# Weight loads of the late blocks, whole and in four pieces

## The chip, the cores and the metric

The kernel runs on one core of a Trainium2 chip, as one launch. The metric is the device time of that launch in microseconds (us); three runs of the kernel before gave 556.94, 559.24 and 561.79 us, median 559.24. The core has five engines that run side by side and meet at semaphores: TensorE (PE, with its weight loads as PEld), VectorE (DVE), ScalarE (ACT), GpSimd (POOL) and SyncE (SP, which here only issues transfers). Transfers run on 16 DMA engines, from two queues that matter here: q1, filled by SP, and q0, filled by POOL.

## The reference

An attention without a score matrix feeds a mixture of experts of which each token uses one. There are 8 batches of 576 tokens, 8 heads of 64, so 4608 tokens of 512 numbers, and 8 experts.

```python
kv = np.einsum('bhsd,bhse->bhde', k_s, v)          # k_s: softmax of k over the tokens
x  = np.einsum('bhsd,bhde->bhse', q_s, kv)         # q_s: softmax of q over its 64 numbers
for b in range(B):                                 # x as (B, S, 512)
    prev_e = -1
    for s in range(S):
        fresh_e = argmax(logits[b, s])             # logits = x @ w_gate
        e = fresh_e if s == 0 or local_gate[b, s] < 0.5 else (prev_e if prev_e >= 0 else fresh_e)
        prev_e = e
        h = np.maximum(x[b, s] @ w1[e], 0.0)       # w1[e]: 512 x 1024, 2 MB in f32
        out[b, s] = p[e] * (h @ w2[e])             # w2[e]: 1024 x 512, 2 MB; p: softmax of logits
```

## The kernel before

Tokens are sorted by expert into blocks of 128 rows, each of one expert. The first NA = 9 blocks hold tokens of the first half and run between pieces of the attention, in an order written out in the table ORDER; the other blocks (b = 9 and up) run one after the other in `block(b)`, from b = 36 on inside nested `If`s that ask whether the block exists. The profile shows some 30 of these late blocks.

A product in f32 is made of f16 pieces: a weight w becomes w1h + w1l (or w2h + w2l), an activation a high and a low part. One block on PE is `ffn1(b,0)`, the second half of the block before (`ffn2(b-1,1)`), `ffn1(b,1)`, `ffn2(b,0)`. `ffn1` stands in an `If` on PE (line 889): a block whose expert has at most 64 rows left in it takes a body with 64 columns, all others the body behind it with 128. So PE jumps once per half. ACT and DVE make the hidden layer's pair (`act_hi`, line 911; `act_lo`, line 915) and POOL gathers rows for block b + 4 (`gather`, 844), the gates (`gather_share`, 850) and scatters the result (`put`, 933). SP turns the rows of block b + 3 by a transposing transfer (`turn_dma`, line 880, tile xT), which needs `prep_lo` (DVE, line 867).

The f32 weights of the next expert wait in two staging tiles of 2 MB, s1 for w1 and s2 for w2. Where a block starts a new expert, `renew(b, pieces)` turns the 16 pieces of 256 KB (128 columns of s1 each, 0 to 7; a 128-row chunk in s2 each, 8 to 15) into the f16 pairs, on ACT (line 190) and DVE (line 955), in an `If` on the flag of the block; otherwise it is jumped over. The pieces 0 to 9 of block b + 1 are renewed during block b (`next_`), 10 to 15 during block b + 1 itself. `fetch(b, i)` is the load of staging tile i with the expert that comes after that of block b; it is issued by SP in every block with a condition (block b starts an expert and another follows), and moves nothing where the condition is 0. In `block(b)` both fetches stand at the end, as 2 MB each: s2 of block b, then s1 of block b + 1. The transfer of s1 for block 9 (`fetch(9, 1)`) is issued from the table ORDER.

SP, like every engine, takes its instructions in order: a transfer whose wait isn't over holds all transfers behind it. On SP each DMA row of the program waits for the engines named behind it (`DVE`, `Activation`) and for earlier transfers (`DMAHW0` to `DMAHW7`, counters that SP's transfers use in turn).

Of the kernel before, what the change touches and what calls it, by code (L numbers as in the profile page):

```python
# [15 lines left out]
ET = mybir.EngineType  # L16
# [4 lines left out]
NE = 8  # L21
# [9 lines left out]
NBM = NBF + NE - 1  # L31
NA = 9
NB = NBM - NA
NP = NA
# [121 lines left out]
def moe_kernel(ctx, tc, q, k, v, w_gate, w_local, w1, w2, out, dbg=None):  # L156
    nc = tc.nc
# [11 lines left out]
    W, plan = {}, []  # L169
# [10 lines left out]
    def at(pair, b):  # L180

        return pair[0][:, b] if b < NA else pair[1][:, b - NA]
# [614 lines left out]

    outr = out.rearrange("b s d -> (b s) d")
    xg, xn, x2, xT, pb, pt, py, hi, lo, ys, ph = ([] for _ in range(11))
    fst, e0, few, phs = {}, {}, {}, {}  # L800
    AHEAD, NPB = 4, 4

    def turns(pool, to, n, shape, dt, name):
# [33 lines left out]
    def word(w_, hi_, engines):  # L837
        return nc.values_load(w_, min_val=0, max_val=hi_, engines=engines,
                              skip_runtime_bounds_check_because="clamped where it is worked out")

    def gather(b):
        src = xrows[0:2 * 1152, :] if b < NA else xrows
        i_, j_ = (gidx[0], b) if b < NA else (gidx[1], b - NA)
        nc.gpsimd.indirect_dma_start(out=xg[b % AHEAD], out_offset=None, in_=src,  # L844
                                     in_offset=bass.IndirectOffsetOnAxis(ap=i_[:, j_:j_ + 1], axis=0))

    def gather_share(b):
        src = shares[0:2 * 1152, :] if b < NA else shares
        i_, j_ = (gidx[0], b) if b < NA else (gidx[1], b - NA)
        nc.gpsimd.indirect_dma_start(out=pb[b % NPB], out_offset=None, in_=src,  # L850
                                     in_offset=bass.IndirectOffsetOnAxis(ap=i_[:, j_:j_ + 1], axis=0))
# [7 lines left out]
    def prep_hi(b):  # L859
        copy(on("Ph", b) if ("Ph", b) in plan[0].tasks else nc.scalar, x2[b % 2][:, 0, :], xn[b % 2], XS)  # L860

    def prep_lo(b):
        if ("Pl", b) in plan[0].tasks and on("Pl", b) is nc.gpsimd:
            nc.gpsimd.tensor_scalar(out=xn[b % 2], in0=xn[b % 2], scalar1=XS, scalar2=None, op0=ALU.mult)
            nc.gpsimd.tensor_tensor(out=x2[b % 2][:, 1, :], in0=xn[b % 2], in1=x2[b % 2][:, 0, :], op=ALU.subtract)
        else:
            nc.vector.scalar_tensor_tensor(out=x2[b % 2][:, 1, :], in0=xn[b % 2], scalar=XS, in1=x2[b % 2][:, 0, :],  # L867
                                           op0=ALU.mult, op1=ALU.subtract)
# [10 lines left out]
    def turn_dma(b):  # L879
        nc.sync.dma_start(out=xT[b % 4].rearrange("p i c t -> p (i c) t"), in_=x2[b % 2].rearrange("p i d -> p (i d)"),  # L880
                          transpose=True)

    def ffn1(b, g):
        if b < NA:
            hidden(b, g, P)
            return
        if g == 0:
            few[0] = word(at(info, b)[:, 5:6], 1, [ET.PE])
        with tc.If(few[0] == 1) as cmp:
            hidden(b, g, P // 2)  # L890
        with cmp.Else():
            hidden(b, g, P)
# [25 lines left out]
    def result(b):  # L918

        return py[0 if b < NP else (b - NP + 1) % 2]  # L920

    def ffn2(b, g):
        hi_, lo_ = hi[b % 2], lo[b % 2]
        for f in range(4 * g, 4 * g + 4):
            for i, (h_, w_) in enumerate(((hi_, W["w2h"]), (hi_, W["w2l"]), (lo_, W["w2h"]))):
                nc.tensor.matmul(result(b), h_[:, f, :], w_[:, f, :], start=(f == 0 and i == 0), stop=(f == 7 and i == 2))  # L926

    def give(b):
        nc.scalar.activation(ys[b % 2], result(b), AF.Copy, scale=pb[b % NPB])

    def put(b):
        i_, j_ = (sidx[0], b) if b < NA else (sidx[1], b - NA)
        nc.gpsimd.indirect_dma_start(out=outr, out_offset=bass.IndirectOffsetOnAxis(ap=i_[:, j_:j_ + 1], axis=0),  # L933
                                     in_=ys[b % 2], in_offset=None, bounds_check=NT - 1, oob_is_err=False)
# [8 lines left out]
    def cut_hi(i, eng=None):  # L943
        s_, h_, _ = piece(i)
        copy(eng or on("Wh", i), h_, s_, WS)

    def cut_lo(i, eng=None):
        s_, h_, l_ = piece(i)
        if (eng or on("Wl", i)) is nc.gpsimd:
            sh = list(s_.shape)  # L950
            nc.gpsimd.tensor_tensor(out=s_, in0=s_, in1=wsc.unsqueeze(2).to_broadcast(sh) if i < 8 else wsc.to_broadcast(sh),
                                    op=ALU.mult)
            nc.gpsimd.tensor_tensor(out=l_, in0=s_, in1=h_, op=ALU.subtract)
        else:
            nc.vector.scalar_tensor_tensor(out=l_, in0=s_, scalar=WS, in1=h_, op0=ALU.mult, op1=ALU.subtract)
# [11 lines left out]
    def flag(b):  # L967
        fst[b] = word(at(info, b)[:, 0:1], 1, [ET.Activation, ET.DVE])

    def renew(b, pieces):  # L970
        with tc.If(fst[b] == 1):  # L971
            for i in pieces:
                cut_hi(i, nc.scalar)
                cut_lo(i, nc.vector)
# [3 lines left out]
            flag(b)  # L978
        renew(b, range(4 * k, 4 * k + 4))

    def fetch(b, i):

        if b >= NBM - 1:
            return
        s_, src = ((W["s1"], w1_src), (W["s2"], w2_src))[i - 1]
        w_ = at(info, b)
        cond, e = w_[:, 4:5], w_[:, 1:2]
        if NX0 <= b < NA:
            cond, e = w_[:, 2:3] if b == NX0 else w_[:, 0:1], w_[:, 3:4]
        kw = dict(cond=(word(cond, 1, [ET.SP]) == 1), cond_hint=False)  # L990
        nc.sync.dma_start(out=s_, in_=src(bass.ds(word(e, NE - 1, [ET.SP]), 1)), **kw)

    pl = Plan(dict(kt=NKT, vt=NVT, km=2, mt=2, kb=2, vp=2, pk=1, psq=2, px=1, pz=2, qt=NQT, qs=3, qe=NQE, xt=NXT, kvT=2, rs=3, cs=1,
                   qm=3, ex=2, xg=AHEAD, xn=2, x2=2, xT=4, pst=1, psh=2, psy=1, hh=2, y=2, dl=1, pb=NPB),
# [92 lines left out]
    for b in range(NP + 4):  # L1087
# [17 lines left out]
        if b > 0:  # L1105
            for i in range(2 if b == NP else 4):
                src = [("F1", b - 1, 0), ("F1", b - 1, 1), ("F2", b - 1, 0), ("F2", b - 1, 1)][i]
                add(("RN", b, i), ACT, renew4, after=[src, ("aj",) if b < NA else ("bj",)], order=[("s1" if i < 2 else "s2", b - 1)])
            add(("s1", b), SP, lambda b: fetch(b, 1), after=[("RN", b, 0), ("RN", b, 1)] + ([("bj",)] if b >= NX0 else []))
        else:  # L1110
            add(("s1", b), SP, lambda b: fetch(b, 1), after=[("Wl", i) for i in range(8)] + [("aj",)], order=[("W", 3)])
        if b == NP:
            continue
        add(("s2", b), SP, lambda b: fetch(b, 2),
            after=([("RN", b, 2), ("RN", b, 3)] if b else [("Wl", i) for i in range(8, 16)] + [("aj",)]) + ([("bj",)] if b >= NX0 else []))
        for g in range(2):
# [15 lines left out]
    def prep_a(b):  # L1132
        if b < NBM:
            prep_x(b)

    def prep_b(b):
        if b < NBM:
            prep_hi(b)
            prep_lo(b)

    def act(b, g):
        act_hi(b, g)
        act_lo(b, g)

    def next_(b, pieces):
        if b + 1 < NBM:
            renew(b + 1, pieces)

    def block(b):


        if b + AHEAD < NBM:
            gather(b + AHEAD)
        prep_a(b + 3)
        if b + 1 < NBM:
            gather_share(b + 1)
            if b + 1 not in fst:
                flag(b + 1)
        ffn1(b, 0)
        act(b, 0)  # L1160
        renew(b, FROM[b][0])
        next_(b, (0, 1))
        ffn2(b - 1, 1)
        ffn1(b, 1)
        give(b - 1)
        put(b - 1)
        renew(b, FROM[b][1])
        next_(b, (2, 3))
        prep_b(b + 3)
        act(b, 1)  # L1170
        renew(b, FROM[b][2])
        next_(b, (4, 5, 6, 7))
        ffn2(b, 0)
        if b + 3 < NBM:
            turn_dma(b + 3)
        fetch(b, 2)
        if b + 1 < NBM:
            fetch(b + 1, 1)
        next_(b, (8, 9))


    FROM = {b: ((10, 11), (12, 13), (14, 15)) for b in range(NBM)}
# [2 lines left out]
    for b in range(NP, NBF):  # L1185
        block(b)

    def rest(b):

        if b < NBM:  # L1190
            used = word(at(info, b)[:, 3:4], 1, [ET.Activation, ET.DVE, ET.PE, ET.Pool, ET.SP])
            with tc.If(used == 0) as cmp:  # L1192
                last(b - 1)
            with cmp.Else():
                block(b)
                rest(b + 1)
        else:
            last(b - 1)
# [34 lines left out]
```

## Time and profile before

| | |
|---|---|
| median of three runs | 559.24 us (556.94 to 561.79) |
| the profiled execution | 556.77 us, of which 555.1 us are its span |
| PE busy | 496.4 us, 89% of the span |
| DVE, ACT, POOL busy | 50%, 40%, 47% |
| mean granted TensorE clock | 0.967 of full |
| bytes moved | 98.63 MB, mean 178 GB/s |

PE is busy 40 of 50 us in 100 to 150 us and nearly without a gap from 150 us on, except for the stretch 235 to 275 us. The late blocks start near 237 us. A new expert is renewed four times in them: from 230, 292, 344 and 394 us (ACT's casts w1h<-s, 32 of them after 225 us, 8 for each). Times in rows are microseconds from the start of the span. In a line "X <- Y" of idle time, X waited for Y; "issue" is idle time for which the profile shows no semaphore wait. The letter q behind an engine (SPq, PEldq) marks its sequencer: branches, register work and the issue of transfers.

### The profile page before, as it was taken

To read this page: it belongs to the slowest core of one execution; us is meant where nothing else is said; L and a number is where in the kernel's file an instruction comes from. 1 tells how busy PE (TensorE), PEld (TensorE's weight loads), DVE (VectorE), ACT (ScalarE), POOL (GpSimd) and SP (SyncE) were. 2 spreads that over 40 slices of the span, in tenths; PEclk is the share of its full clock that TensorE was granted. 3 is DMA by queue.
4 is the path that set the end of the run, shared out by engine and by line. 5 is a ranking of instruction groups with operands and counts; after the bars stand their busy time and mean duration, and the time that the engine had idled before them with its cause. 6 is when DMAs were issued, how large, how long until landed. Compare 5 with 4: busy or idle time off the path is not lost. (4 is left out here: it accounts for less than half of the span.)

```text
span 555.1 us, 18417 instructions
## 1 busy us (share of the span) xinstructions
PE 496.4 (89%) x7298; PEld 368.4 (66%) x7298; DVE 275.6 (50%) x501; ACT 221.0 (40%) x388; POOL 259.3 (47%) x284
## 2 busy tenths in 40 slices
PE   1667796768999999988799999999999999999995
PEld 0556675656776777665677677777677777677672
DVE  6879797899654773572117412831471111211210
ACT  1446576897321343441117323712552222222221
POOL 3666885457725341585234523532534423523431
PEclk9988896998899999989899999999999999999999
DMA  8998899398341459389724893795388432443532
GB/s 312 376 375 295 265 324 378 127 343 275 67 101 61 124 182 319 118 205 225 141 52 129 282 143 63 216 246 83 91 238 218 95 87 63 113 74 62 97 91 52
DMA packets 79398, 98.63 MB, mean 178 GB/s; under 512 B 46623, under 2 KB 54815, under 8 KB 79264
## 3 DMA queue, kind: packets, MB, share of 16 engines
q1 hardware_dynamic: 71616, 74.66, 47.0%
q0 software_dynamic: 7648, 22.20, 15.9%
q8 instruction: 82, 1.34, 1.1%
q14 instruction: 52, 0.43, 0.3%
HBM read 206.76 MB, written 20.89 MB: 410 GB/s over the span
## 5 line engine op out<-in xcount | busy, mean ns | idle before, releaser
L903 PE MATMUL ph<-xT,w1h 128*128 128x128 f16 (+1 forms) x2432 | 183.0, 219 | 3.4 <-issue 3.4
L903 PEld LDWEIGHTS <-w1h 128*128 128x128 f16 x2432 | 147.2, 99 | 3.5 <-issue 3.5
L915 DVE SCALAR_TENSOR_TENSOR lo<-ph,hi 128x512 f16<-128x512 f32 x76 | 52.3, 689 | 142.9 <-ACTq L971 135.8
L906 PE MATMUL ph<-xT,w1l 128*128 128x128 f16 (+1 forms) x1216 | 116.5, 219 | 5.8 <-issue 3.0
L933 POOL DMA_INDIRECT out<-y,sidx x38 | 39.8, 1046 | 175.1 <-ACTq L971 141.1
L911 ACT ACTIVATE hi<-ph 128x512 f16<-128x512 f32 x76 | 45.2, 595 | 179.3 <-PE ph L903 179.3
L906 PEld LDWEIGHTS <-w1l 128*128 128x128 f16 x1216 | 82.8, 99 | 23.9 <-issue 3.7
L926 PEld LDWEIGHTS <-hi 128*128 128x128 f16 x608 | 56.2, 98 | 54.5 <-issue 0.3
L926 PE MATMUL py<-w2h,hi 128*128 128x512 f16 x184 | 70.0, 381 | 0.0
L926 PE MATMUL py<-w2l,hi 128*128 128x512 f16 x184 | 69.9, 380 | 0.0
L926 PE MATMUL py<-w2h,lo 128*128 128x512 f16 x184 | 69.7, 379 | 0.0
L867 DVE SCALAR_TENSOR_TENSOR x<-xn,x 128x512 f16<-128x512 f32 x37 | 30.3, 818 | 70.7 <-ACT x L190 65.1
L844 POOL DMA_INDIRECT xg<-xrows,gidx x42 | 46.3, 1103 | 23.8 <-DVE tz L679 12.1
L926 PEld LDWEIGHTS <-lo 128*128 128x128 f16 x304 | 29.8, 98 | 36.0 <-issue 0.3
L850 POOL DMA_INDIRECT pb<-shares,gidx x39 | 42.6, 1091 | 8.3 <-issue 7.8
L926 PE MATMUL pi<-w2h,hi 128*128 128x512 f16 x120 | 45.5, 379 | 0.0
L926 PE MATMUL pi<-w2l,hi 128*128 128x512 f16 x120 | 45.5, 379 | 0.0
L926 PE MATMUL pi<-w2h,lo 128*128 128x512 f16 x120 | 45.5, 379 | 0.0
L431 POOL TENSOR_TENSOR qs<-qt,qm 128x512 f32<-128x512 f32 x33 | 35.9, 1098 | 19.5 <-PE pq L440 17.7
L855 POOL TENSOR_TENSOR xn<-xg 128x512 f32<-128x512 f32 x35 | 36.9, 1057 | 13.6 <-DMA xg<-xrows,gidx 7.5
L322 DVE TENSOR_REDUCE KM<-KT 128x128 f32<-128x1152 f32 x16 | 34.4, 2161 | 4.0 <-DMA KT<-in_k 4.0
L455 PE MATMUL px<-R,qe 64*64 64x74 f32 x864 | 23.4, 249 | 11.1 <-ACT xt L190 4.4
(219 smaller groups left out, 585.9 us busy)
## 6 DMA issues: line engine op xcount, KB each, us to landing
s<-in_moe_w SPq DMA_DIRECT2D x77, 2048.0 KB
xrows<-xt SPq DMA_DIRECT2D x12, 888.0 KB
KT<-in_k SPq DMA_DIRECT2D x16, 576.0 KB
VT<-in_v SPq DMA_DIRECT2D x16, 576.0 KB
qt<-in_q SPq DMA_DIRECT2D x8, 640.0 KB
qt<-in_q SPq DMA_DIRECT2D x8, 512.0 KB
s<-in_moe_w SPq DMA_DIRECT2D x4, 1024.0 KB
xg<-xrows,gidx POOLq DMA_INDIRECT x42, 5.2
```

Source lines behind the costliest of these rows:

```text
L322: nc.vector.tensor_reduce(out=KM[b % 2][:, 2 * u:2 * u + 2], in_=KT[b % NKT][:, u:KG:2].rearrange("p g c d -> p g d c"), axis=AX.X, op=ALU ...
L431: on("qs", t, c).tensor_tensor(out=qs[t, c].rearrange("p (g x) d -> p g x d", x=2), in0=qt[t, u][:, :, i, :].rearrange("p (x g) d -> p g x ...
L844: nc.gpsimd.indirect_dma_start(out=xg[b % AHEAD], out_offset=None, in_=src, in_offset=bass.IndirectOffsetOnAxis(ap=i_[:, j_:j_ + 1], axis=0))
L850: nc.gpsimd.indirect_dma_start(out=pb[b % NPB], out_offset=None, in_=src, in_offset=bass.IndirectOffsetOnAxis(ap=i_[:, j_:j_ + 1], axis=0))
L855: eng.tensor_tensor(out=xn[b % 2].rearrange("p (g x d) -> p g x d", g=4, x=2), in0=xg[b % AHEAD].rearrange("p (g x) -> p g x", g=4)[:, :, ...
L867: nc.vector.scalar_tensor_tensor(out=x2[b % 2][:, 1, :], in0=xn[b % 2], scalar=XS, in1=x2[b % 2][:, 0, :], op0=ALU.mult, op1=ALU.subtract)
L903: nc.tensor.matmul(ph_[:, f, 0:n], W["w1h"][:, c, fs], xT_[:, i, c, 0:n], start=False, stop=(c == 3 and i == 1))
L906: nc.tensor.matmul(ph_[:, f, 0:n], W["w1l"][:, c, fs], xT_[:, 0, c, 0:n], start=(c == 0), stop=False)
L911: nc.scalar.activation(hi[b % 2][:, 4 * g:4 * g + 4, :], phs[g], AF.Relu)
L915: nc.vector.scalar_tensor_tensor(out=lo[b % 2][:, gs_, :], in0=phs[g], scalar=0.0, in1=hi[b % 2][:, gs_, :], op0=ALU.max, op1=ALU.subtract)
L926: nc.tensor.matmul(result(b), h_[:, f, :], w_[:, f, :], start=(f == 0 and i == 0), stop=(f == 7 and i == 2))
L933: nc.gpsimd.indirect_dma_start(out=outr, out_offset=bass.IndirectOffsetOnAxis(ap=i_[:, j_:j_ + 1], axis=0), in_=ys[b % 2], in_offset=None, ...
```

## The change

In the late blocks `fetch` takes a list of parts. A part n is columns 256 n to 256 n + 255 of s1 (that is pieces 2 n and 2 n + 1), or row chunks 2 n and 2 n + 1 of s2 (pieces 8 + 2 n and 9 + 2 n), 512 KB. `block(b)` issues each part behind the `renew` that used up its pieces, and in block 9 the parts 0 and 1 of s2 together. The words for condition and expert are read once per block and kept (`due`) where they were read for each fetch. Loads in the first 9 blocks, and s1 for block 9, stay whole.

```diff
-    def fetch(b, i):
+    def fetch(b, i, parts=None):
...
-        kw = dict(cond=(word(cond, 1, [ET.SP]) == 1), cond_hint=False)
-        nc.sync.dma_start(out=s_, in_=src(bass.ds(word(e, NE - 1, [ET.SP]), 1)), **kw)
+        if b not in due:
+            due[b] = word(cond, 1, [ET.SP]), word(e, NE - 1, [ET.SP])
+        cond, e = due[b]
+        for n in ((None,) if parts is None else parts):
+            s_, src = ((W["s1"], w1_src), (W["s2"], w2_src))[i - 1]
+            s_, src = s_[:], src(bass.ds(e, 1))
+            if n is not None:
+                at_ = (slice(None), slice(None), slice(256 * n, 256 * n + 256)) if i == 1 else (slice(None), slice(2 * n, 2 * n + 2))
+                s_, src = s_[at_], src[at_]
+            nc.sync.dma_start(out=s_, in_=src, cond=(cond == 1), cond_hint=False)
...
         renew(b, FROM[b][0])
+        fetch(b, 2, (0, 1) if b == NP else (1,))
         next_(b, (0, 1))
+        fetch(b + 1, 1, (0,))
         ffn2(b - 1, 1)
         ffn1(b, 1)
         give(b - 1)
         put(b - 1)
         renew(b, FROM[b][1])
+        fetch(b, 2, (2,))
         next_(b, (2, 3))
+        fetch(b + 1, 1, (1,))
         prep_b(b + 3)
         act(b, 1)
         renew(b, FROM[b][2])
         next_(b, (4, 5, 6, 7))
+        fetch(b, 2, (3,))
+        fetch(b + 1, 1, (2, 3))
         ffn2(b, 0)
         if b + 3 < NBM:
             turn_dma(b + 3)
-        fetch(b, 2)
-        if b + 1 < NBM:
-            fetch(b + 1, 1)
         next_(b, (8, 9))
+        fetch(b + 1, 2, (0,))
```

SP in block 9, before. xT3 is the tile of block 11, xT0 that of block 12; s1_1934 and s2_1935 are the staging tiles:

```order
L880 DMA_TRANSPOSE xT3_1960<-x21_1956 128x8x128 [waits DVE_49,Pool_49]
L971 UNCONDITIONAL_BRANCH x4
L880 DMA_TRANSPOSE xT0_1957<-x20_1955 128x8x128 [waits DVE_49,PE_49]
L971 UNCONDITIONAL_BRANCH x2
L889 UNCONDITIONAL_BRANCH
L838 TENSOR_LOAD info34_78 x2
L991 REGISTER_ALU x2
L991 ISA
L991 DMA s2_1935<-in_moe_w2 128x8x512 [waits DMAHW4_49,DVE_49,Activation_49]
```

The same place on SP in the changed kernel:

```order
L880 DMA_TRANSPOSE xT3_1960<-x21_1956 128x8x128 [waits DVE_49,Pool_49]
...
L998 DMA s2_1935<-in_moe_w2 128x2x512 [waits DMAHW4_49,DVE_49,Activation_49]
...
L998 DMA s2_1935<-in_moe_w2 128x2x512 [waits DVE_49,Activation_49]
...
L838 TENSOR_LOAD info34_78 x2
...
L998 DMA s1_1934<-in_moe_w1 128x4x256 [waits DMAHW7_49,DVE_49,Activation_49]
...
L998 DMA s2_1935<-in_moe_w2 128x2x512 [waits DVE_49,Activation_49]
...
L998 DMA s1_1934<-in_moe_w1 128x4x256 [waits DMAHW5_49,DVE_49,Activation_49]
...
L998 DMA s2_1935<-in_moe_w2 128x2x512 [waits DMAHW6_49,DVE_49,Activation_49]
...
L880 DMA_TRANSPOSE xT0_1957<-x20_1955 128x8x128 [waits DMAHW1_49,PE_49]
```

The turn of block 12 stood ahead of the load of s2 and stands behind all four parts of it now, and behind the four parts of s1 for block 10, of which the first waits for DMAHW7, the whole load of s1 that block 9 issued.

SP in an ordinary late block, before (xT2 is the tile of block 14):

```order
L880 DMA_TRANSPOSE xT2_1959<-x20_1955 128x8x128 [waits DVE_49,PE_49]
L971 UNCONDITIONAL_BRANCH x2
L889 UNCONDITIONAL_BRANCH
L838 TENSOR_LOAD info34_78 x2
...
L991 DMA s2_1935<-in_moe_w2 128x8x512 [waits DMAHW0_49,DMAHW5_49,DVE_49,Activation_49]
L838 TENSOR_LOAD info34_78 x2
...
L991 DMA s1_1934<-in_moe_w1 128x4x1024 [waits DMAHW1_49,DMAHW6_49,DVE_49,Activation_49]
```

And in the changed kernel, the block's last five of eight loads and its turn:

```order
L998 DMA s2_1935<-in_moe_w2 128x2x512 [waits DMAHW0_49,DVE_49,Activation_49]
L889 UNCONDITIONAL_BRANCH
...
L998 DMA s1_1934<-in_moe_w1 128x4x256 [waits DMAHW1_49,DVE_49,Activation_49]
...
L998 DMA s1_1934<-in_moe_w1 128x4x256 [waits DMAHW2_49,DVE_49,Activation_49]
L880 DMA_TRANSPOSE xT2_1959<-x20_1955 128x8x128 [waits DMAHW3_49,PE_49]
...
L998 DMA s2_1935<-in_moe_w2 128x2x512 [waits DMAHW4_49,DVE_49,Activation_49]
```

Of a block's loads all but the last now stand ahead of its turn, where both stood behind it.

## Rows read from the trace of the kernel before

**Rows 1.** Windows by stage: busy us (count) per engine, granted clock, DMA share, GB/s
```profile
core 0: us, PE busy (x) PEld busy (x) DVE busy (x) ACT busy (x) POOL busy (x), PEclk, DMA share, GB/s
250.00:300.00 50.00, 43.90 (x524) 31.94 (x521) 13.73 (x22) 14.31 (x24) 20.80 (x20) 0.97 0.67 133
350.00:400.00 50.00, 50.00 (x602) 35.89 (x600) 20.73 (x30) 19.94 (x35) 20.17 (x20) 1.00 0.69 166
```

**Rows 2.** Windows of finer stretches, columns as in rows 1
```profile
249.50:258.00 8.50, 6.95 (x85) 5.14 (x84) 2.42 (x4) 1.61 (x4) 3.54 (x4) 1.00 1.13 134
258.00:267.00 9.00, 7.81 (x94) 5.67 (x92) 1.52 (x3) 1.50 (x3) 4.85 (x5) 1.00 1.13 303
267.00:274.00 7.00, 3.64 (x35) 2.57 (x34) 1.25 (x2) 1.32 (x2) 0.73 (x1) 0.93 0.67 95
241.50:249.50 8.00, 8.00 (x73) 4.99 (x71) 5.91 (x9) 6.54 (x12) 6.98 (x7) 0.95 1.04 276
```

**Rows 3.** Timeline of PE, 268.5 to 277 us: start, us, instruction
```profile
268.63 0.39 PE L906 MATMUL ph<-xT,w1l 128*128 128x128 f16 x4
...
269.30 0.39 PE L906 MATMUL ph<-xT,w1l 128*128 128x128 f16 x4
273.05 1.01 PE L903 MATMUL ph<-xT,w1h 128*128 128x128 f16 x8 [3.36 <-issue]
...
276.41 0.39 PE L926 MATMUL pi<-w2h,hi 128*128 128x512 f16 x1
```

**Rows 4.** PE's branch of line 889, in 245:258, 258:264, 420:520: ns min/median/max
```profile
L889 PEldq COMPARE_BRANCH  x2: 355/2458/4562, 247.2 to 252.1; - x2
L889 PEldq COMPARE_BRANCH  x1: 3778/3778/3778, 259.5 to 259.5; - x1
L889 PEldq COMPARE_BRANCH  x19: 205/216/2425, 424.3 to 519.2; - x19
```

**Rows 5.** Timeline of SP, 236 to 275 us
```profile
240.28 0.39 SPq L991 DMA_DIRECT2D s<-in_moe_w  x1
242.94 7.80 SPq L880 DMA_TRANSPOSE xT<-x  x2
252.75 1.51 SPq L991 DMA_DIRECT2D s<-in_moe_w  x2
259.11 4.39 SPq L880 DMA_TRANSPOSE xT<-x  x1
```

**Rows 6.** DMA queues, 430 to 520 us: share of 16 engines, then issues
```profile
q0 software_dynamic: 1728, 5.09, 22.9%
q1 hardware_dynamic: 9504, 2.36, 17.3%
...
xT<-x SPq DMA_TRANSPOSE x9
```

**Rows 7.** DMA queues, 302.6 to 309.2 us: packets, MB, share of 16 engines
```profile
q1 hardware_dynamic: 522, 2.08, 87.5%
```

**Rows 8.** Timeline of DVE, 242 to 252 us: the halves w2l of block 9
```profile
242.93 2.49 DVE L955 SCALAR_TENSOR_TENSOR w2l<-s,w2h 128x512 f16<-128x512 f32 x4
...
249.95 1.28 DVE L955 SCALAR_TENSOR_TENSOR w2l<-s,w2h 128x512 f16<-128x512 f32 x2
```

**Rows 9.** Timeline of SP: an ordinary late block, and two loads at the start
```profile
440.56 1.24 SPq L880 DMA_TRANSPOSE xT<-x  x1
443.64 1.24 SPq L991 DMA_DIRECT2D s<-in_moe_w  x2
451.10 1.24 SPq L880 DMA_TRANSPOSE xT<-x  x1
...
113.11 1.39 SPq L963 DMA_DIRECT2D s<-in_moe_w  x2
```

**Rows 10.** Windows 14 to 28 us; the page's transfer of that stretch
```profile
14.00:28.00 14.00, 9.03 (x254) 7.47 (x255) 12.38 (x12) 5.90 (x8) 9.32 (x12) 1.00 1.07 376
...
KT<-in_k SPq DMA_DIRECT2D x16, 576.0 KB
```

More of the change, by code (lines that the diff above doesn't have):

```diff
@@ L799, in moe_kernel @@
     xg, xn, x2, xT, pb, pt, py, hi, lo, ys, ph = ([] for _ in range(11))
-    fst, e0, few, phs = {}, {}, {}, {}
+    fst, e0, due, few, phs = {}, {}, {}, {}, {}
     AHEAD, NPB = 4, 4
@@ L979, in renew4 @@
         renew(b, range(4 * k, 4 * k + 4))
-    def fetch(b, i):
+    def fetch(b, i, parts=None):
         if b >= NBM - 1:
             return
-        s_, src = ((W["s1"], w1_src), (W["s2"], w2_src))[i - 1]
         w_ = at(info, b)
```

## Prediction

> **What bounds the kernel now.** I read the windows by stage first, to find where PE, the busiest engine, is not busy. From 150 us on it is full (50.00 of 50 us in the window from 350 us) except from 250 to 300 us, where 6.10 us are missing [rows 1]. That decides what the change can give: the late blocks are bound by PE, and loads that PE never waits for are worth nothing however early they come. Weights for a switch of expert are asked for at the switch before it, some 50 us ahead, so no PE instruction waits for them.
>
> So what are the 6.10 us? The finer windows put them in three places: 1.55 us in 249.5 to 258, 1.19 in 258 to 267, 3.36 in 267 to 274 [rows 2], and PE is idle there for "issue", with no semaphore that the profile shows. The first two are seen in PE's own sequencer: its branch of line 889 takes 216 ns in the middle, but 4,562 ns at 252.1 us and 3,778 ns at 259.5 us [rows 4]. From 252.10 the long branch lasts to 256.66 us, and PE starts again there; its array had work queued for the first 3 us of it. In the quiet stretch from 430 us a long one takes at most 2,425 ns [rows 4], and costs PE nothing. The third gap, 269.69 to 273.05 us, is in the middle of straight code [rows 3]. I read all three as PE waiting for its own instructions, which come by the same DMA engines as the data. That is an inference: the rows show the late branch and the idle "issue", not the cause.
>
> What the DMA engines do there supports it. They are full from 241.5 to 267 us (share 1.04, 1.13, 1.13), but in 249.5 to 258 us they move 134 GB/s, against 276 and 303 in the neighbours [rows 2]. SP's timeline tells what is in that stretch [rows 5]: the load of s1 (2 MB) from 240.28 us, two turns issued in the 7.80 us from 242.94 us, then s2 (2 MB) from 252.75 us, then a turn whose issue alone takes 4.39 us. Two turns and POOL's gathers behind a 2 MB load are what the slow window holds.
>
> PE pays once more: after the third gap the granted clock is down, and 32 matmuls from 273.05 to 276.41 us take 3.36 us [rows 3]. Before the gap 12 took 269.30 - 268.63 = 0.67 us, so 32 take 1.79. The clock costs 1.57 us. **All that the change can win is 6.10 + 1.57 = 7.67 us.**
>
> **The change part by part.** *Words read once per block, more loads on SP.* Eight loads stand in a block where two stood. A load that moves nothing costs SP at most half of 1.24 us, which two of them took together, reads of the words included, and at least some 0.1 us: two real loads without such reads went out in 1.39 us, most of it their own issue [rows 9]. With 1.24 us for the turn a block costs SP between 8 x 0.1 + 1.24 = 2.0 and 8 x 0.62 + 1.24 = 6.2 us. A block lasts 451.10 - 440.56 = 10.54 us [rows 9]. SP keeps up in either case, so I take 0. If it did not, the turn would come late first.
>
> *The turn stands behind seven loads.* In an ordinary block it then waits until DVE and ACT are past the pieces 14, 15 and 4 to 7, some 2 to 3 us later than now. It turns rows for three blocks on, over 20 us ahead. It delays PE by 0; if that cover went, `ffn1` of block b + 3 would wait. It also no longer goes out together with POOL's gather. Worth 0 in a quiet block, since PE is full there.
>
> *Block 9, s2.* DVE ends pieces 8 to 11 at 242.93 + 2.49 = 245.4 us and the last pair at 249.95 + 1.28 = 251.2 us [rows 8]. Parts 0 and 1 go out at some 245.5 us. Then SP meets the first part of s1 for block 10. It moves nothing, but waits for the whole load of s1 that block 9 issued: 276 GB/s over 8 us from 241.5 us is 2.2 MB [rows 2], so it lands near 250 us. Part 2 is ready at 248.5 and goes out at some 250.5; part 3 at 251.4 us. So the words "as soon as" hold for half of this load. Its data lie behind the whole of s1 in the queue of SP in any case: some 250 to 260 us, where s2 came after 252.75 us and behind two turns before.
>
> *Block 9, the turn of block 12* goes out after part 0 has landed, near 253 us, and its data come behind part 3, near 260 us. Its rows are needed at `ffn1(12,0)`, which follows the 12 matmuls of `ffn2` that begin at 276.41 us [rows 3], so near 279. That is a slack of some 19 us; I take 0. The buffer that it reads is written again by ACT one and a half blocks later; if that cover went, ACT would wait there and PE behind it.
>
> *When the DMA engines come free* decides the third gap. In the quiet stretch a block's turn costs 90 x 17.3% / 9 = 1.73 us of all 16 engines, and POOL's transfers 90 x 22.9% / 9 = 2.29 us [rows 6]; a 2 MB load costs 6.6 x 87.5% = 5.8 us [rows 7]. Two loads, three turns and three blocks of POOL's transfers come to 11.6 + 5.2 + 6.9 = 23.7 us, which from 241.5 us ends at 265.2. The windows before hold 1.04 x 8 + 1.13 x 8.5 + 1.13 x 9 + 0.67 x 7 = 32.8 us, to 274 us [rows 2]. The 9 us between are what turns and gathers lose to each other. With one turn, then s2, then one turn, I expect about half of this back: free near 267 to 269 us, just ahead of the third gap. I take that gap and its clock as gone: 3.36 + 1.57 = 4.93 us. Bounds: 0 and 4.93.
>
> *The first two gaps* lie beside the load of s2 as before, but with one turn instead of two. Bounds 0 and 2.74 us; I take half, 1.37.
>
> *The three later switches* (292, 344, 394 us). There each part of s1 and s2 goes out by itself over some 20 us. PE has nothing to win: 50.00 of 50 us already [rows 1]. It can lose where a branch meets a part, as at 252 us; below I bound it by 0, above by one gap of 3.36 + 1.57 us at each, 14.8. I take 0.6 in all, near the lower end, because the same 4 MB moves there now in two bursts without such a gap.
>
> One rule speaks against the cut. The Trainium skill ("DMA: Bandwidth & Descriptors", Bandwidth) wants at least 1 MiB in one transfer and gives 2.0 us + bytes / 436 GB/s for one alone; by it four parts would take 12.8 us for 6.8, an estimate. This kernel's trace disagrees: transfers of 576 KB, one behind the other, moved 376 GB/s from 14 to 28 us [rows 10]. What follows from the rule is the slower rival below.
>
> Sum: -4.93 - 1.37 + 0.6 = -5.7 us. The profiled execution, 556.77 us (a span of 555.1 and 1.7 around it), would become 551.1. It is 2.5 us below the median of the three runs, 559.24; I hang the difference on the median: **553.5 us**.
>
> **Rivals.** *A, as above:* the third gap goes. For it: that gap comes when SP's queue drains last, and s2 is moved 8 us ahead. 553.5 us (own range 549 to 557).
>
> *B, the order moves, the gaps stay.* The bytes are the same, the engines are full from 241.5 us in both kernels, and PE's instructions must come through somewhere. The parts may just delay another branch. For it: the first two gaps lie beside turns that s1 alone holds up. Against it: the slow window is the one with two turns. 559.2 us, 557 to 562.
>
> *C, it doesn't do what it says:* SP sits at the part that waits for s1's landing, all of s2 follows in one burst, the turn of block 13 gets behind it and the late end stays at 274 us. The two later parts do go out together by my reckoning. Then only the first gaps change: 558 us.
>
> *D, slower:* four small transfers keep the engines busy longer than one large one, and at the later switches PE's instructions meet turns, gathers and parts at once over 20 us instead of 13. If two of three switches get a gap of 4.93 us and block 9 gains nothing, it is 559.2 + 9.9 = 569 us; one alone with no gain, 564. It decides where parts move below some half of 376 GB/s, so that the next part's wait for its place is never over. That is the rule's mechanism. Against it stand the rows of 576 KB.
>
> **How the numbers follow.** 1% of 559.24 is 5.6 us: faster means below 553.6, slower above 564.8, about what a measurement of this kernel tells from no change. Chances: A 0.57, B 0.22, C 0.09, D 0.12. A's centre lies just past the bound of 1%; its far end, all 7.67 us and the 2.5 by which the slower runs may hold longer gaps, is 549. Two thirds of A are faster, 0.38; the rest of A, B, C and a sixth of D are the same, 0.52; the rest of D is slower, 0.10. The range leaves out the far side of D and a little under A: 548.0 to 563.0.
>
> **What would show it.** PE busy in 250 to 300 us up from 43.90 to 48 or more, or the same three gaps (B). PE's branch of line 889 below 3.5 us everywhere in 245 to 265 us. SP: parts 0 and 1 at 245.5, parts 2 and 3 close together after 250 us, the next turn near 253 us. The DMA share below 0.5 from 269 us instead of 274. PE at 49.5 of 50 us or more from 300 to 450 us; less there is D. The forecast is wrong if PE waits for anything but its own instructions in the three gaps, or if they stay at that place with the engines free.

## The result and the profile after

The changed kernel takes 552.95 us in the median of 21 runs (547.3 to 558.2), the kernel before, beside it, 557.29 us in 21 (551.25 to 561.81). The ratio is **0.9917, interval 0.9888 to 0.9945**, so some 4.6 us less. Ratios, here and below, are taken over the runs in the faster of the two states that each kernel shows. In a later session the same program was timed again: 0.9921 (0.9884 to 0.9958). That is a gain, though a little under the 1% that I had set as the bound of "faster".

The profiled execution has a span of 549.7 us where before had 555.1. The windows of the changed kernel, first the stage, then the fine stretches (busy us and count for PE, PEld, DVE, ACT and POOL, then granted clock, DMA share, GB/s):

```profile
250.00:300.00 50.00, 48.03 (x591) 34.66 (x589) 18.71 (x28) 19.00 (x33) 21.34 (x21) 1.00 0.66 170
249.50:258.00 8.50, 7.03 (x85) 5.13 (x84) 2.82 (x5) 1.99 (x4) 4.03 (x4) 1.00 0.96 235
258.00:267.00 9.00, 8.50 (x98) 6.00 (x95) 1.39 (x2) 1.19 (x2) 4.05 (x4) 1.00 0.91 224
267.00:274.00 7.00, 7.00 (x80) 4.99 (x79) 1.38 (x2) 1.92 (x3) 4.10 (x4) 1.00 0.45 122
```

Against [rows 1, 2] PE has 48.03 busy us rather than 43.90. The 3.36 us that were missing in 267 to 274 are all back, and the clock is at 1.00 there (2.4 GHz) where it was 0.93. The first gap is still 1.47 us, the second 0.50. The slow stretch 249.5 to 258 moves 235 GB/s instead of 134, and from 267 us the engines are mostly free (0.45 against 0.67).

The branch of line 889 after, in 245 to 258 and in 258 to 264 us (ns min/median/max; [rows 4] has those of before):

```profile
L889 PEldq COMPARE_BRANCH  x2: 355/2416/4476, 247.4 to 252.2; - x2
L889 PEldq COMPARE_BRANCH  x1: 2902/2902/2902, 259.8 to 259.8; - x1
```

The long branch at 252 us is as long as before, 4,476 ns, where I had forecast less than 3.5 us everywhere; the next one is 0.9 us shorter. SP's timeline after (start, us taken by the issues, count), to be read beside [rows 5]:

```profile
240.41 0.38 SPq L998 DMA_DIRECT2D s<-in_moe_w  x1
243.08 4.06 SPq L880 DMA_TRANSPOSE xT<-x  x1
247.77 7.61 SPq L998 DMA_DIRECT2D s<-in_moe_w  x8
258.02 1.25 SPq L880 DMA_TRANSPOSE xT<-x  x1
260.55 5.40 SPq L998 DMA_DIRECT2D s<-in_moe_w  x8
266.04 1.27 SPq L880 DMA_TRANSPOSE xT<-x  x1
```

One turn goes out before s2 now and not two; the turn of block 12 goes at 258.02 and that of block 13 at 266.04 us, where before the turn of block 13 went at 259.11, into the load of s2.

**A measure that is finer than the total.** The part of the program ahead of the change varies by itself: PE's wait for the first w1l of block 9 ended between 231.3 and 240.0 us in the 14 profiles that I have, though the loads up to there are the same. From that wait on PE is busy nearly all the time, so a shift of block times shows PE's stalls and the clock. I therefore compare two stretches of every profile: *stretch 1*, from the end of the wait for w1l to the first branch of block 12 (blocks 9 to 11), and *stretch 2*, from that branch to the end of PE's last matmul. For the kernel before, stretch 1 goes from 237.54 to 276.20 us and takes 38.66 us, stretch 2 272.41.

| kernel | stretch 1 | stretch 2 | ratio (interval) |
|---|---|---|---|
| before, two profiles | 38.66, 34.97 | 272.41, 272.17 | 1 |
| changed, two profiles | 33.08, 34.22 | 271.66, 271.61 | 0.9917, 0.9921 |
| e1 quarters in block 9 only | 32.39 | 272.84 | 0.9957 (0.9926 to 0.9987) |
| e2 quarters from block 10 on only | 34.64 | 271.62 | 0.9950 (0.9915 to 0.9985) |
| e3 whole loads ahead of the turn | 34.92 | 276.15 | 0.9999 (0.9960 to 1.0038) |
| e4 quarters behind the turn | 36.00 | 271.61 | 0.9948 (0.9909 to 0.9987) |
| e7 before without s2 of block 9 | 36.29 | 272.54 | 0.9931 (0.9894 to 0.9967) |
| e9 turn of block 13 behind the loads | 35.99 | 272.26 | 1.0023 (0.9963 to 1.0084) |
| e5 before, no branch in blocks 9 to 11 | 31.06 | 273.79 | 0.9942 (0.9915 to 0.9969) |
| e6, e11 changed, no such branch | 31.04, 30.98 | 272.24, 271.32 | 0.9892 (0.9852 to 0.9932), 0.9877 (0.9821 to 0.9933) |
| e12 = e9 and no such branch | 30.91 | 272.70 | 0.9897 (0.9858 to 0.9937) |

Each stretch is a single execution. The two of before differ by 3.7 us in stretch 1, so a difference of 1 or 2 us there says nothing by itself. The clock adds to it: in 13 of the 14 profiles the granted clock falls for 3.4 us at the start of stretch 1, and the first half of block 9 takes 6.77 to 6.92 us; in e1 it does not fall, and that half takes 5.28.

### The profile page after: what moved, and what is told of

Read it like the earlier page. It is cut to its first block, busy times and chain, and to the rows that moved or that the text cites. A ratio compares the mean times of both kernels' runs of the same rounds, so it can differ in the third digit from the quotient of the medians.

```text
span 549.7 us, 19358 instructions
## 1 busy us (share of the span) xinstructions
PE 493.6 (90%) x7298; PEld 366.2 (67%) x7298; DVE 276.2 (50%) x501; ACT 220.7 (40%) x388; POOL 258.1 (47%) x284
## 5 line engine op out<-in xcount | busy, mean ns | idle before, releaser
L903 PE MATMUL ph<-xT,w1h 128*128 128x128 f16 (+1 forms) x2432 | 181.0, 218 | 0.5 <-issue 0.5
L903 PEld LDWEIGHTS <-w1h 128*128 128x128 f16 x2432 | 145.4, 98 | 0.7 <-issue 0.6
L867 DVE SCALAR_TENSOR_TENSOR x<-xn,x 128x512 f16<-128x512 f32 x37 | 31.6, 853 | 69.1 <-ACT x L190 65.2
L850 POOL DMA_INDIRECT pb<-shares,gidx x39 | 41.5, 1065 | 8.3 <-issue 8.2
```

The source lines that it names most:

```text
L903: nc.tensor.matmul(ph_[:, f, 0:n], W["w1h"][:, c, fs], xT_[:, i, c, 0:n], start=False, stop=(c == 3 and i == 1))
```

## The experiments

### One half of the change, and size against order

My theory T was that the gain is made in block 9, by the order; its rivals were S (the size of the transfers) and L (the late blocks).

**e1** takes the quarter loads in block 9 alone (`if b == NP:` ahead of each part), and from block 10 on:

```diff
+        if b > NP:
+            fetch(b, 2)
+            fetch(b + 1, 1)
```

> Block 9 issues its quarter loads as the change does; from block 10 on, whole loads behind the turn as in the kernel before. Theory T (the gain is made in block 9 alone: s2 of block 9 goes out early and the turn of block 12 leaves behind it, so the DMA engines are drained before 267 us and PE's third gap with its 1.57 us of half clock is gone): ratio 0.991 to 0.993, PE at least 48.0 of 50 us in 250 to 300. Rival S (the size of 512 KB lets PE's instructions through): the same in block 9, so also 0.992. Rival L (the gain is spread over the later blocks, where turn and gather stand apart): 0.998 to 1.000, third gap of 3 us still there or only half gone.

Measured: 551.21 us, ratio 0.9957. The third gap is gone, as T says. Stretch 1 is the shortest of the kernels that keep the branch, 32.39 us, but some 1.6 us of that is the clock at its start, up to which e1 does not differ from the changed kernel. The ratio is only half the gain, and stretch 2 has a stall that the changed kernel has not. The waits of PE in 225 to 545 us (line waited for, us in total, times, longest):

```profile
PE ph L906 <- issue: 1.6, 1, 1.6
PE ph L906 <- DVEq L971: 1.2, 1, 1.2
PE ph L903 <- issue: 1.1, 1, 1.1
```

The first two are the two gaps behind the branches; the last, 1.1 us in straight code, came at 372 us.

**e2** is the other half: block 9 as before, quarters from block 10 on (`if b > NP:` ahead of each part, and for block 9 the whole loads behind the turn).

> Block 9 loads whole tiles behind the turn as in the kernel before; from block 10 on, quarter loads as the change has them. T and S: ratio 0.999 to 1.000, all three gaps of PE between 250 and 275 us still there (PE 43.5 to 44 of 50 us in 250 to 300). Rival L: 0.992, and the later part of the program shorter by 4 us.

Measured: 551.05 us, ratio 0.9950. T and S, which expected no gain, are both wrong here, and L expected more. The third gap is gone too, though block 9 is the old one: the two gaps behind the branches are all that is left ("issue: 3.5, 2, 2.1"). SP shows what differs:

```profile
251.81 21.33 SPq L998 DMA_DIRECT2D s<-in_moe_w  x10
273.24 1.28 SPq L880 DMA_TRANSPOSE xT<-x  x1
```

The parts of block 10 stand ahead of its turn, the turn of block 13. It goes out at 273.24 us, long after s2 has landed, where before it went at 259.11 into that load. So what the kernels without the gap share up to here is not a moved turn of block 12, as I had thought, but a moved turn of block 13: either half of the change brings it to the end of that load or past it (in e1 it is the second of two turns that hold SP from 259.68 to 265.8 us). The two halves' gains, 0.43% and 0.50%, add up to about the whole, 0.83%; with intervals of 0.3% each that is no proof of a sum.

**e3** changes the order alone, with whole loads:

```diff
         next_(b, (4, 5, 6, 7))
+        fetch(b, 2)
+        fetch(b + 1, 1)
         ffn2(b, 0)
```

> Order alone: both loads stay whole (2 MB each), but are issued ahead of the turn in every block rather than behind it. T: s2 of block 9 goes out only some 3 us earlier than before, but still ahead of the turn of block 12, which is what keeps the engines from two loads and a turn at once; ratio 0.992 to 0.995, third gap gone or under 1 us. Rival S: 0.999 to 1.001, third gap as before.

Measured: 553.68 us, ratio 0.9999. No gain. The third gap is gone, as T expected, but PE loses the time elsewhere:

```profile
PE pi L926 <- issue: 2.8, 2, 2.5
PE ph L906 <- DVE w1l L955: 2.6, 1, 2.6
PE ph L906 <- issue: 2.3, 1, 2.3
PE ph L903 <- issue: 1.1, 2, 0.8
```

The first gap is 2.35 us, and there is a stall of 2.52 us at 319 us, which with two smaller ones makes stretch 2 the longest of all, 276.15 us.

**e4** changes the size alone, in the old order behind the turn: `fetch(b, 2, (0, 1, 2, 3))` and `fetch(b + 1, 1, (0, 1, 2, 3))`.

> Size alone: each load is cut into four of 512 KB, but all four are issued one after the other behind the turn, where the kernel before issues the whole load. T: 0.999 to 1.002, third gap of 2.5 to 3.5 us still there, since the bytes ask for the engines at the same time as before. Rival S: 0.992, third gap gone though the order is the old one.

Measured: 551.57 us, ratio 0.9948. T expected nothing, S more. Stretch 1, 36.00 us, lies between the two of before: the third gap is not there, though the turn of block 13 goes out at 254.95 us, into the load of s2 (issued from 245.53 us), and holds SP for 3.47 us. The two gaps ahead of it are 1.21 and 2.05 us, so that PE comes later to the place, which may be why; that was not tested. Stretch 2 is 271.61 us, that of the changed kernel. What size alone wins is seen in the late blocks of this profile, not in its block 9.

By the times, then, order alone wins nothing (e3, 0.9999) and size alone some half of the gain (e4, 0.9948). That speaks for S more than for T, though the third gap is gone in both. All four keep the words that are read once per block; by e3 that alone gains nothing either.

### Is the third gap part of the kernel before?

All four kernels had lost the third gap, those too that should have kept it. So **e8** is the kernel before, unchanged, for a second profile.

> The kernel before, unchanged, for a second profile of it. Theory T1 (the third gap of PE, in block 10, belongs to the order of the kernel before): again some 3 us of idle PE in straight code 13 to 16 us after the first of the three, followed by half clock; from the end of the wait for w1l to PE's last matmul again 310 to 312 us. Rival R (a PE stall in straight code strikes at changing places, since a page of PE's instructions now and then comes late, and the profile of before happened to show one there): no gap there or one at another place, 305 to 308 us from w1l to the end unless another falls in.

The branches place the gap in the second half of block 11 (`ffn1(11,1)`), not in block 10 as that text has it. The second profile (550.21 us) shows it again, at the same place. PE's timeline:

```profile
264.75 0.39 PE L906 MATMUL ph<-xT,w1l 128*128 128x128 f16 x4
267.63 0.61 PE L903 MATMUL ph<-xT,w1h 128*128 128x128 f16 x8 [2.50 <-issue]
```

The half block took 8.48 us here and 10.48 in the first profile; 5.67 in both of the changed kernel, 5.67 to 6.10 in e1 to e4, and 5.68 in e7 and e9. So it belongs to the kernel before, by 2 of 2 against 0 of 8 profiles with the same branch, and both times it stands ahead of the same matmul, the 17th of that half. Its price is 2.8 to 4.8 us, clock included; the half clock that T1 expected behind it did not come in this execution. The first two gaps were only 0.30 and 0.75 us here: the first is 0.3 to 3.7 us over the ten profiles with the branch. So from the wait for w1l to PE's last matmul this execution took 307.15 us, not the 310 to 312 that T1 gave, and in the range that R gave. T1 had the place right and the time wrong.

### Whose instructions?

If the gaps are PE's missing instructions, PE must be helped by code that needs fewer of them. In **e5** (kernel before) and **e6** (changed kernel) PE's branch is left out of blocks 9 to 11, where it always went to the 128-column body:

```diff
-        if b < NA:
+        if b < NA + 3:
             hidden(b, g, P)
             return
```

> The kernel before with PE's branch on the number of rows taken out of blocks 9 to 11, where the trace shows that it always goes to the 128-row half: PE's code there is straight, and half as long. If the first two gaps (1.55 and 1.19 us) are PE's jump waiting for its instructions, both go: 2.5 us, ratio 0.995; and if the third one is tied to the page after the second jump, it goes too: 0.986. If PE is short of instructions there whatever their order (full DMA engines), gaps of the same size stay in straight code: 0.999 to 1.001.

> The changed kernel with the same branch taken out of blocks 9 to 11. The two gaps that are left there (1.47 and 0.50 us) go if they are the jump's: 0.988 against the kernel before, 0.996 against the changed one. If they are the full engines': as the changed kernel, 0.992.

Measured: e5 551.28 us, ratio 0.9942; e6 547.5 us, 0.9892. **All three gaps are gone in both**, whatever the loads do, and stretch 1 falls to 31.06 and 31.04 us. The waits of PE in 225 to 545 us, of e5:

```profile
PE ph L906 <- DVE w1l L955: 2.6, 1, 2.6
PE ph L903 <- issue: 2.2, 1, 2.2
```

and of e6:

```profile
PE ph L906 <- DVE w1l L955: 2.6, 1, 2.6
PE ph L906 <- issue: 0.4, 1, 0.4
```

The 2.2 us of e5 are a new stall in straight code, at 374 us, behind whole loads; it is part of why e5 gained 0.6% and not the 1.4% of my larger number. e6's 0.9892 is near the 0.988 that I expected.

The profile also shows the late instructions themselves. Queue q8, "instruction", carries packets of 16 KB. Over the span there are 82 of them in each of the ten kernels and repeats that keep the branch, and 79 in each of the four that leave PE's branch and second body out of three blocks. Before and e5:

```profile
q8 instruction: 82, 1.34, 1.1%
q8 instruction: 79, 1.29, 1.1%
```

The other instruction queue, q14, has 52 packets in both. So q8 carries PE's code. And the gaps end with its pages: behind 240 us the 14 profiles have 30 gaps of PE over 0.25 us, and 28 of them end 1.28 to 1.61 us after a packet of q8 landed (the other two 2.05 us after), where a page lands every 6 us or so. The first gap of before ends 1.42 us after such a landing, the second 1.42 and the third 1.44.

The page that ends the third gap comes late. It lands 9.7 us after the page ahead of it in the first profile of before and 8.8 us in the second; the same page lands 4.2 to 7.1 us after in the eight other profiles with the branch, each time before PE needs it. The 7.1 us are those of e4, where the turn of block 13 still meets the load. The queues of the kernel before in 262 to 270 us (packets, MB, share of 16 engines), the 8 us that lead into the third gap:

```profile
q1 hardware_dynamic: 1381, 1.10, 63.3%
q0 software_dynamic: 195, 0.54, 49.9%
q14 instruction: 1, 0.01, 0.2%
```

and of the changed kernel in the same 8 us:

```profile
q1 hardware_dynamic: 1646, 0.42, 26.3%
q0 software_dynamic: 192, 0.57, 17.9%
q8 instruction: 2, 0.03, 1.5%
q14 instruction: 3, 0.02, 0.9%
```

Before, no page comes in these 8 us; the next one is in 270 to 272 us (one packet on q8, landed at 271.6), and PE goes on at 273.05 us. After, the same number of small packets of POOL (q0) takes a third of the time, and two pages come. Full engines alone are not the reason. The 16 engines' busy share in 40 slices of those 8 us, before and in e9 (below), where nothing but the turn of block 13 is moved away, and e9's queues:

```profile
DMA  9998999999998979990110130004958958797999
DMA  9999999999999999999999767640000000000000
q1 hardware_dynamic: 676, 1.35, 46.1%
q0 software_dynamic: 224, 0.57, 18.3%
q8 instruction: 2, 0.03, 1.7%
```

Before, the engines are nearly idle from 265.6 to 267.4 us and no page comes there; in e9 they are full for 4.4 us and a page comes in the midst of that (262.7 to 263.8 us), another at 267.3 us. What is missing in e9 is the turn (1024 packets of 256 B): 112 packets under 512 B against 1031. So these rows, of one execution each, point to the turn beside the load. How a turn would hold up a page they do not show.

e5 keeps the turn where before has it, and no page comes either, in 262.6 to 270.3 us:

```profile
q1 hardware_dynamic: 1443, 1.23, 59.4%
q0 software_dynamic: 193, 0.56, 47.4%
q14 instruction: 1, 0.01, 0.3%
```

but PE does not stop, presumably since its code without the second body is shorter and the pages it has last longer (three pages less over three blocks).

**e7** takes the suspected load away instead: the kernel before, with `if b > NP:` ahead of `fetch(b, 2)`.

> The kernel before without the load of w2 in block 9 (2 MB are not moved, so one expert is computed with the w2 of another). If PE's three gaps come from DMA engines full of that load beside turn and gather, the second and third gap go (they lie during and after it), the first, before it lands, stays: 4 to 6 us, ratio 0.989 to 0.993. If the load has no part in them: 0.999 to 1.001 and all gaps stay.

Measured: 550.68 us, ratio 0.9931, at the near end of what was expected, and the second and third gap are gone. But the first one was 3.73 us, so stretch 1 is 36.29 us, inside the spread of before, and its profile doesn't confirm the ratio; the profiled execution, 557.41 us, was the longest of the ten. In this one profile the first gap comes without the load, and the later two do not.

### One instruction moved, and the best version

**e9** moves in the kernel before only the turn that block 10 issues (that of block 13) behind that block's two loads.

```diff
-        if b + 3 < NBM:
+        if b + 3 < NBM and b != NP + 1:
             turn_dma(b + 3)
         fetch(b, 2)
         if b + 1 < NBM:
             fetch(b + 1, 1)
+        if b == NP + 1:
+            turn_dma(b + 3)
```

> The kernel before, with one instruction moved: in block 10 the turn of block 13 is issued behind that block's two loads rather than ahead of them; all loads whole. Theory T (the third gap comes from this turn and the gather beside it, which meet the load of w2 of block 9 on the DMA engines, so that PE's next page of instructions comes late): the turn goes out after 268 us, when that load has landed, the third gap and its half clock are gone, the first two stay; 4 us less, ratio 0.992 to 0.994, block 10's second half to block 11's first branch 5.7 us rather than 8.5 to 10.5. If it is the size of the loads that makes the gap: gap as before, 0.999 to 1.001.

Measured: 553.1 us, ratio 1.0023. The third gap is gone, as T expected, and the gain is not there. The turn went out at 270.69 us, together with the next one, and block 11's second half took 5.68 us: no third gap. But the first gap was 2.81 us in this execution, ahead of anything that the edit moves, and the clock fell behind it:

```profile
256.00:262.00 6.00, 4.38 (x49) 4.38 (x50) 0.69 (x1) 0.63 (x1) 4.66 (x5) 0.72 1.13 215
```

The interval excludes the 0.992 to 0.994 that I expected. So taking the third gap away by the order wins no time that can be measured, here as in e3. A longer first gap could hide it; that this is the rule in e9 was not tested.

**e10** is the changed kernel again, **e11** is e6 again, and **e12** joins e9's order to the missing branch, with no quarter load at all.

> The changed kernel again, for a second profile and beside the next two. T: no gap in block 10, one gap of 0.3 to 2 us behind each of the two branches, ratio 0.992. PE's stalls after 300 us: none over 0.5 us if quarter loads keep the page's way free there, as in its first profile; 1 to 2.5 us at one place if they strike by chance, as they did in the first and third of the runs with whole loads in the late blocks.

> The changed kernel without PE's branch in blocks 9 to 11, again, beside the changed kernel alone. All three gaps gone: 0.988 to 0.990 against the kernel before, 1 to 2.5 us under the changed kernel of this call. If the branch is worth nothing beside the new order: the same as the changed kernel within 0.1%.

> The kernel before with the turn of block 13 behind the loads and without PE's branch in blocks 9 to 11, and no quarter load at all. If the three gaps are all that the quarter loads win back: as the changed kernel without the branch, 0.987 to 0.990. If the quarter loads are worth something after block 12 as well (PE's stalls of 1 to 2.5 us after 300 us with whole loads): 0.991 to 0.994, with such a stall in the profile.

Measured: e10 549.59 us, 0.9921, with two gaps (2.0 and 1.1 us) behind the branches, none in the second half of block 11, none after 300 us. e11 547.85 us, 0.9877 (I had expected 0.988 to 0.990), with no gap of PE at all behind the wait for w1l:

```profile
PE ph L906 <- DVE w1l L955: 2.6, 1, 2.6
```

e12 548.32 us, 0.9897, with its one stall at 370 us:

```profile
PE ph L906 <- DVE w1l L955: 2.6, 1, 2.6
PE ph L903 <- issue: 1.2, 1, 1.2
```

The changed kernel without the branch is the fastest version measured: 1.74 us under e10 in the median, and 2.0 to 3.2 us in stretch 1. The intervals of e10 and e11 overlap, so the trace carries that difference more than the clock time does. e12 lies within the interval of e11: once PE has its straight code, the times cannot tell quarter loads from whole ones. Its ratio is that of my first reading (the three gaps are all that quarter loads win back), its stall that of my second. The traces put 1.3 us between the two, nearly all of it in stretch 2.

**What the late blocks gain** shows when stretch 2 is sorted. With quarter loads from block 10 on (changed twice, e2, e4, e6, e11) it is 271.3 to 272.2 us, five of six below 271.7. With whole loads (before twice, e1, e3, e5, e7, e9, e12) it is 272.2 to 276.2 us. Stalls of PE for "issue" after 300 us, of 0.3 us and more: seven of the eight profiles with whole loads have one, 0.31 to 2.52 us; of the six with quarters one, 0.36 us. The places repeat: the first branch of block 17 in both profiles of before and in e7; the second half of block 21 in e1, e3, e5 and e12, ahead of its 8th matmul in e1 and e3, and of its 48th in e5 and e12, where PE's code ahead is shorter. So these stalls, like the third gap, belong to places in PE's code.

## Why the prediction was right, and where not

553.5 us against a median of 559.24 is a ratio of 0.990; 0.992 was measured. What A describes is seen in the profiles: the third gap goes. That this is what the times gained is not shown: e3 and e9 lose the same gap and gain nothing, and of the kernels that keep the branch and all loads only those with quarter loads gain (e1, e2, e4 and the changed kernel, 0.4 to 0.8%). That the total came out near has luck in it, since two of the three terms have the wrong sign and, as measured, cancel (+0.6 and -0.65 us). The 552.95 us lie so close to 553.5 also because the kernel before took 557.29 us beside them, not 559.24. By A's steps:

- *All that can be won is PE's missing time in 250 to 300 us.* Right for blocks 9 to 11 of the profile that I read: without the branch they take 31 us, 7.6 to 7.8 less than there, where I had 7.67. Against the second profile of before it is 3.9 to 4.1. And the later blocks, which lose only 0.31 us in the profile that I read (300 to 350 us), lose up to 3.6 us in other kernels with whole loads.
- *PE waits for its own instructions.* Held up by e5, e6, e11 and e12, where PE's code is shortened, the bytes stay and all three gaps go whatever the order of the loads, and by the pages of q8 with which the gaps end. It is no longer only read from "issue".
- *The third gap and its clock go, -4.93 us.* Right in place: half block 11 falls from 10.48 and 8.48 us to 5.67, so -4.8 against the profile that I used and -3.8 against the mean of two. The 1.57 us of clock are not in the second profile. The reason that I gave, engines free a little earlier, is too simple: in e9 a page comes while the engines are full, and what is missing there is the turn.
- *The first two gaps lose half, -1.37 us.* Wrong. They are 1.47 + 0.50 and 2.0 + 1.1 us after, 1.55 + 1.19 and 0.30 + 0.75 before: no gain, and by the means of two 0.6 us more. One turn instead of two went out ahead of s2, as I had it, but the page with which the first gap ends came no sooner: 17.7 and 18.2 us into stretch 1 after, 17.8 and 15.9 before. I had taken the halves from one execution; their spread is as large as the term.
- *The later switches cost 0.6 us.* Wrong in sign. Stretch 2 falls by 0.5 to 0.8 us against before's two, and by about 1 us against the median of all profiles with whole loads. Rival D had it that parts spread over 20 us meet more of PE's branches. In the changed kernel they cost PE nothing: it is at 150.00 of 150 us from 300 to 450, where before is at 149.69.
- *SP's times.* The turn of block 11 took 4.06 us to issue, so parts 0 and 1 went out at 247.8, not 245.5, and the turn of block 12 at 258.0, not 253. The size of the delay was missed, not the order. In e9's profile the third gap goes with the turn after it, which I had not named for A and which C had down as a danger: in the changed kernel it goes out at 266.04 us, past the load.
- *Extra loads on SP, and a later turn: 0.* Right; PE waits for no turn.
- *Four transfers of 512 KB for one of 2 MB.* Size costs nothing here: e4, the cut alone in the old order, is 0.5% faster than before, not slower. That agrees with the 376 GB/s of [rows 10] and not with the rule of at least 1 MiB in one transfer (the Trainium skill, "DMA: Bandwidth & Descriptors", Bandwidth), which is measured there on transfers issued from GpSimd, where these are SP's. The formula that I took from the Trainium skill stands in another section of "DMA: Bandwidth & Descriptors", "Anatomy of one DMA — SWDGE (gpsimd) path", and is fitted on such transfers too.

Sum by the traces (means of two): -3.8 for the third gap and +0.6 for the others in stretch 1, -0.65 in stretch 2, so -3.8 us; by the times -4.6 (-6.2 to -3.1). What of the difference lies ahead of block 9 stays open, and so does how much of the measured gain is the third gap's.

## What to carry to other kernels

When the busiest engine idles for "issue" and its branches grow long, look at the instruction queues of the profile in those microseconds. A stall that ends shortly after a page has landed (here 1.3 to 1.6 us) is most likely a wait for code. Then the cheapest cure may be less code (a branch and a body that this place never needs): that gave the lowest times here. Keeping a turn out of a large load took one stall away in e9, but no time. Take a second profile before pricing a stall: here the place repeated, the size did not, and in e3 the time won at one place was lost at another.

## What the chip showed that I had not expected

- A page of 16 KB on q8 can come several us late: it landed 9.7 and 8.8 us after the page ahead of it in the two profiles of before, 4.2 to 7.1 in eight others. PE then stopped in straight code, without a branch near it, for 3.36 and 2.50 us, and went on some 1.4 us after the page had landed.
- Issuing a turn holds SP for 1.24 us in a quiet block ([rows 9]) and for 3.47 us (e4) to 6.92 us (e3, at 250.49 us) beside a load of 2 MB.
- POOL's 195 packets (0.54 MB) took 49.9% of 16 engines over 8 us beside a turn and the end of a large load; 224 packets (0.57 MB) took 18.3% beside such a load without the turn (e9).
